# Local-window attention with a gated MLP on one core: the scores of two head pairs made by four 64x64 products a block

## The chip, the cores and the metric

The kernel runs on one core of one Trainium2 chip. The metric is the device time of one execution in microseconds (us). TensorE (PE) does the matrix products, VectorE (DVE) and ScalarE (ACT) the elementwise work, GpSimd (POOL) a little of it, and SyncE (SP) issues the loads and stores.

## The reference

Everything is fp32 in HBM. B = 4 batches, H = 8 heads, S = 768 positions, D = 64, DM = 512, DF = 512.

```python
# attention: a band of +-15 positions, and 24 block summaries (block = 32)
k_sum = k.reshape(B, H, 24, 32, D).max(axis=3)
v_sum = v.reshape(B, H, 24, 32, D).mean(axis=3)
scores_l = scale * q @ k.T                   # masked to |i - j| < 16
scores_s = scale * q @ k_sum.T + log(32)     # all 24 summaries
a = softmax(concat[scores_l, scores_s])
x = a @ concat[v, v_sum]                     # heads side by side: (B, S, 512)
# MLP with a spatial gate
h = relu(x @ w_in); u, v = h[..., :512], h[..., 512:]
v_n = (v - mean(v)) / sqrt(var(v) + 1e-6)    # over the 512 features
v_s = w_spatial @ v_n + b_spatial            # over the 768 positions
out = (u * v_s) @ w_out
```

## The kernel before

**Attention.** A query block is 64 positions (QB), and it sees KW = 120 columns: 64 + 32 keys around it and the 24 summaries, which lie in the key tile beside each segment. A unit of work is one batch, one chunk of 256 positions (four blocks, BPU) and one pair of heads; two units make a group, so that there are 4 x 3 x 2 = 24 groups. A pair's queries and keys lie one head in partitions 0 to 63 and the other in 64 to 127. Each unit goes through these steps:

- `scores` (product at L410): for each of four blocks and each head `a`, a product of 64 query rows (the stationary operand) with 120 key columns. Head `a` uses rows 64a to 64a+63 of TensorE's array and, since its output goes to PSUM partitions 64a to 64a+63, the same columns. So a unit has eight products, on two of the array's four 64x64 quarters, and fills one PSUM bank (tile `s`, 480 of 512 columns). Two such tiles exist (`s=2` in `SLOTS`).
- softmax: per block a DVE operation (L419: mask, scale, row minimum; it is listed with the read of its accumulator) and an ACT exponential (L423); then the sums' inverse (L428, L429) and a scaling of the whole tile (L431, on DVE or POOL).
- `trans` (L442): four transposes into tile `t`, copied to `pt` (L229, on ACT or DVE).
- `mix` (L458): for a whole group, 16 products of the values `ve` with the transposed weights, 64x64 each, in tile `x`. ACT makes the rounded high part `xh` (L471), DVE the remainder `xl` (L472).

**The MLP.** Each fp32 operand is a sum of two parts that TensorE takes at full rate, high and low, and each product is three (`mm3`, L491). In the order of a batch: `pv` (the half of `w_in` that is normalised) for six row tiles, `pu` (the other half) for four column tiles and two position ranges, `sp` (the spatial product) for four column tiles and two position ranges, and `po` (output) for six row tiles. DVE, ACT and POOL split the weights `win` (L262 to L284), `wsp` (L242, L243) and `wo` during batch 0, normalise `pv` (L518 to L530, result `vnh`, `vnl`) and gate `sp` (L553, L554, L562, L563; results `gt`, `gu`), which `po` reads.

**What sets the order.** Nothing is scheduled by hand on the engines. Each step is given to a planner (`Plan.add`) with its engines, an estimated duration, a priority and what it reads and writes. `Plan.order` picks, again and again, the operation that can start first (ties by priority) and so writes one order for each engine, which the engines keep. Tiles with few buffers (`SLOTS`) are handed out in turn (`TURNS`). Attention groups have priorities a `PACE` apart, the MLP's pieces follow each other from `DENSE_0` on, and the weights' priorities are `WIN_V`, `WIN_U`, `WSP_AT` and `WO_AT`. `FAVOUR` and `BUSY` say how long and how strongly POOL is preferred to DVE. While TensorE waits by the plan, before a marked point in group 1, the kernel fills in small `warm` products (L662).

Of the kernel before, what the change touches and what calls it, by code (L numbers as in the profile page):

```python
# [9 lines left out]
F32 = mybir.dt.float32  # L10
# [10 lines left out]
P = 128  # L21
# [4 lines left out]
QB = 64  # L26
# [37 lines left out]
class Plan:  # L64


    SLOTS = dict(s=2, t=1, x=1, m=4, k=4, vt=1, p=4, pt=3, x01h=2, x01l=2, x2h=2, x2l=2, g=NG, e=3, u=1, vnh=1, vnl=1,
                 gm=2, st=8, bs=4, mv=4)
    TURNS = ("s", "t", "x", "k", "vt", "p", "pt", "gm", "e")
    LAG = dict(PE=250, ACT=150, DVE=150, POOL=150, SP=0)  # L70

    def __init__(self):
# [106 lines left out]
def tile_local_summary_attention_gmlp(ctx: ExitStack, tc: tile.TileContext, qT, kext, vpad, vnat, vT, w_in, w_sp, b_rep, w_out, maskc, out):  # L179
# [39 lines left out]
    def early(name):  # L219
        return EARLY.get(name, 0.0)  # L220
# [176 lines left out]

    p_sb, pt_sb = {}, {}

    def scores(u, pri):  # L400
        b, c, pr = u
        ps = Buf(ps_s, [P, 512], F32, "s", f"s{b}_{c}_{pr}")
        kt, (qt, buf) = k_sb[b, pr], q_sb.pop(u)

        def mm(e):
            for i in range(BPU):
                g = c * BPU + i
                for a in range(2):
                    hs = slice(a * D, (a + 1) * D)
                    nc.tensor.matmul(  # L410
                        out=ps.t[hs, i * KW:(i + 1) * KW], lhsT=qt[hs, i], rhs=kt.t[hs, g * SEG:g * SEG + KW],
                        start=True, stop=True)
        add(("PE", 930), mm, pri, w=[ps], r=[kt, f"q{buf}"])
        pt = p_sb[u] = Buf(att, [P, BPU, KW], F32, "p", f"p{b}_{c}_{pr}")
        st = Buf(sums, None, None, "st", f"st{b}_{c}_{pr}")
        for i in range(BPU):
            g = c * BPU + i
            mi = 0 if g == 0 else (2 if g == NSEG - 1 else 1)
            add(("DVE", 205), lambda e, i=i, mi=mi: nc.vector.tensor_tensor_reduce(  # L419
                out=pt.t[:, i, :], in0=ps.t[:, i * KW:(i + 1) * KW], in1=mask[:, mi, :],  # L420
                scale=-1.0 / D ** 0.5, scalar=3e38, op0=ALU.add, op1=ALU.min,
                accum_out=st.t[:, 0, i:i + 1]), pri, w=[(pt, i)], r=[ps, "mask", pt, st])
# [8 lines left out]
        add(dict(DVE=590, POOL=1080), lambda e: eng(e).tensor_tensor(  # L431
            out=pt.t, in0=pt.t, in1=st.t[:, 0, :BPU].unsqueeze(2).broadcast_to([P, BPU, KW]), op=ALU.mult), pri,
            w=[(pt, "n")], r=[(pt, "i"), st, pt], port=True)

    def trans(u, pri):
        b, c, pr = u
        ps = Buf(ps_t, [P, 512], F32, "t", f"t{b}_{c}_{pr}")
        pt = p_sb.pop(u)

        def mm(e):  # L440
            for i in range(BPU):
                nc.tensor.transpose(out=ps.t[:KW, i * P:(i + 1) * P], in_=pt.t[:, i, :], identity=ident)  # L442
        add(("PE", 450), mm, pri, w=[ps], r=[(pt, "n"), pt])
        tt = pt_sb[u] = Buf(att, [KW, BPU * P], F32, "pt", f"pt{b}_{c}_{pr}")
        add(dict(ACT=510, DVE=600), lambda e: copy(e, tt.t, ps.t[:KW]), pri, w=[tt], r=[ps])

    xt, xh, xl, x2 = {}, {}, {}, {}

    def mix(b, c, g, buf, pri):
        ps = Buf(ps_x, [P, 2, CH], F32, "x", f"x{b}_{c}_{g}")  # L450
        tts = [pt_sb.pop((b, c, 2 * g + r)) for r in range(2)]

        def mm(e):
            for r in range(2):
                for n in range(BPU):
                    for a in range(2):
                        o = r * P + a * D
                        nc.tensor.matmul(  # L458
                            out=ps.t[a * D:(a + 1) * D, r, n * QB:(n + 1) * QB],
                            lhsT=ve[buf][:, n, o:o + D],  # L460
                            rhs=tts[r].t[:, n * P + a * QB:n * P + (a + 1) * QB],
                            start=True, stop=True)
        add(("PE", 1300), mm, pri, w=[ps], r=[*tts, f"vea{buf}", f"veb{buf}", f"ves{buf}_0", f"ves{buf}_1"])
        if c == 0:
# [78 lines left out]
    def spatial(b, th, d, pri):  # L543
        s = batch_state(b)
        ps = Buf(ps_m, [P, 512], F32, "m", f"sp{b}_{th}_{d}")
        ts = slice(0, 2 * TH) if th == 0 else slice(2 * TH, S)
        n = ts.stop - ts.start
        ds = slice(d * P, (d + 1) * P)
        vh, vl, u = s["vh"], s["vl"], s["u"]
        mm3(ps, n, [((lambda k=k: vh.t[:, k, ds], lambda k=k: vl.t[:, k, ds], lambda k=k: wsp_h[:, k, ts], lambda k=k: wsp_l[:, k, ts]),  # L550
                     [vh, vl, (vh, k), (vl, k), f"ws{k}_{ts.start}h", f"ws{k}_{ts.start}l"]) for k in range(NT)], pri)
# [3 lines left out]
        gt = Buf(moe, [P, 2 * TH], F32R, "g", f"gt{b}_{th}_{d}")  # L555
# [7 lines left out]
        add(two_ns(n), lambda e: eng(e).tensor_sub(out=gl[1](), in0=g.t[:, :n], in1=gh[1]()), pri, w=[kl], r=[g, kh, gt, gl[0]], port=True)  # L563
        s["gh"][th, d], s["gl"][th, d] = (*gh, kh), (*gl, kl)
# [40 lines left out]
    def attention(i):  # L605
# [68 lines left out]
VT_OFF, VM_OFF, KP_OFF = 7.67, 6.61, -9.44
# [74 lines left out]
```

## Time and profile before

| | |
|---|---|
| median of 3 runs | 435.26 us (435.07 to 436.68) |
| profiled execution, its own time | 436.41 us |
| its span, first to last instruction | 434.6 us |
| TensorE busy | 425.7 us, 98% of the span |
| VectorE busy | 265.6 us, 61% |
| ScalarE busy | 221.7 us, 51% |
| GpSimd busy | 45.6 us, 10% |
| granted TensorE clock, mean | 0.995 |

The busy time of TensorE is that of pipelined products whose ends are modelled, so the distance from one start to the next tells more than a duration. The span lies inside the profiled execution's time; the 1.8 us around it belong to no instruction. Each fp32 product of the code (L410, L458, L363, L662) is two MATMUL instructions in the trace; a transpose (L442) and a product of split operands (L491) is one.

### The profile page before, as it was taken

To read this page: it belongs to the slowest core of one execution; us is meant where nothing else is said; L and a number is where in the kernel's file an instruction comes from. 1 tells how busy PE (TensorE), PEld (TensorE's weight loads), DVE (VectorE), ACT (ScalarE), POOL (GpSimd) and SP (SyncE) were. 2 spreads that over 40 slices of the span, in tenths; PEclk is the share of its full clock that TensorE was granted. 3 is DMA by queue.
4 is the path that set the end of the run, shared out by engine and by line. 5 is a ranking of instruction groups with operands and counts; after the bars stand their busy time and mean duration, and the time that the engine had idled before them with its cause. 6 is when DMAs were issued, how large, how long until landed. Compare 5 with 4: busy or idle time off the path is not lost.

```text
span 434.6 us, 8979 instructions
## 1 busy us (share of the span) xinstructions
PE 425.7 (98%) x3374; PEld 353.7 (81%) x3374; DVE 265.6 (61%) x921; ACT 221.7 (51%) x668; POOL 45.6 (10%) x65
## 2 busy tenths in 40 slices
PE   8979999999999999999999999999999999999996
PEld 7637787788898888888888988789788988898885
DVE  4858999989993948455581657365482437143322
ACT  5658985874574546554273346375263254231121
POOL 1033611210001013010000002100000002010000
PEclk9989999999999999999999999999999999999999
DMA  8998967242155832320143251102103000000021
GB/s 288 362 271 289 296 205 247 76 133 60 26 165 161 250 118 60 106 67 26 38 144 118 87 186 27 38 24 62 38 26 109 26 36 15 0 2 0 2 97 48
DMA packets 25867, 47.03 MB, mean 108 GB/s; under 512 B 2528, under 2 KB 12896, under 8 KB 25696
## 3 DMA queue, kind: packets, MB, share of 16 engines
q1 hardware_dynamic: 25680, 46.33, 33.7%
q8 instruction: 26, 0.43, 0.4%
q14 instruction: 17, 0.14, 0.1%
q10 hardware_dynamic: 144, 0.13, 0.1%
HBM read 40.16 MB, written 6.29 MB: 107 GB/s over the span
## 4 chain that ended last, share of the span: by engine, by line
PE 82%; DMA 8%; DVE 8%; SPq 1%; issue 0%; ACT 0%; ACTq 0%
PE sp L491 24%; PE po L491 15%; PE pu L491 13%; PE pv L491 12%; PE s L410 8%; PE x L458 4%; PE t L442 4%; DMA vn<-in_vnat_dram 3%; DMA k<-in_kext_dram 2%; PE vsum L363 2%; DMA qd<-in_qT_dram 1%; DMA vt<-in_vT_dram 1%; DMA ws<-in_w_sp_dram 1%; DVE gm L342 1%; DVE p L419 1%; DVE p L431 1%
## 5 line engine op out<-in xcount | busy, mean ns | idle before, releaser
L423 ACT ACTIVATE p<-p,sums 128x120 f32<-128x120 f32 x192 | 73.6, 386 | 8.0 <-DVE sums L419 7.8
L491 PE MATMUL sp<-wsp_h,vnh 128*128 128x512 f32 (+1 forms) x192 | 66.7, 348 | 0.0
L491 PE MATMUL sp<-wsp_l,vnh 128*128 128x512 f32 (+1 forms) x192 | 64.7, 337 | 0.0
L491 PE MATMUL sp<-wsp_h,vnl 128*128 128x512 f32 (+1 forms) x192 | 64.6, 336 | 0.0
L419 DVE CUSTOM_DVE_ANT_0 p<-s,mask 128x120 f32<-128x120 f32 x192 | 42.8, 276 | 12.4 <-PE s L410 12.2
L491 PE MATMUL po<-wo_h,gt 128*128 128x512 f32 x128 | 47.7, 402 | 0.0
L410 PE MATMUL s<-k,qd 64*64 64x120 f32 x768 | 45.9, 267 | 0.5 <-DMA qd<-in_qT_dram 0.5
L410 PEld LDWEIGHTS s<-k,qd 64*64 64x64 f32 x768 | 39.1, 133 | 7.7 <-issue 4.4
L491 PE MATMUL pu<-xh,win_h 128*128 128x512 f32 (+1 forms) x128 | 44.7, 349 | 0.0
L491 PE MATMUL pu<-xh,win_l 128*128 128x512 f32 (+1 forms) x128 | 43.1, 337 | 0.0
L491 PE MATMUL pu<-xl,win_h 128*128 128x512 f32 (+1 forms) x128 | 43.1, 336 | 0.0
L562 ACT CAST gt<-g 128x512 fp32r<-128x512 f32 (+1 forms) x32 | 16.3, 513 | 50.2 <-DVE g L554 50.1
L491 PEld LDWEIGHTS sp<-wsp_h,vnh 128*128 128x128 f32 x192 | 36.4, 189 | 5.1 <-issue 1.3
L491 PE MATMUL pv<-win_h,xh 128*128 128x512 f32 x96 | 39.8, 414 | 0.0
L491 PEld LDWEIGHTS sp<-wsp_h,vnl 128*128 128x128 f32 x192 | 36.4, 189 | 3.9
L472 DVE TENSOR_TENSOR xl<-x,xh 128x512 fp32r<-128x512 f32 x24 | 16.4, 685 | 37.7 <-ACT xh L471 37.7
L491 PEld LDWEIGHTS sp<-wsp_l,vnh 128*128 128x128 f32 x192 | 36.4, 190 | 3.5
L491 PE MATMUL pv<-win_l,xh 128*128 128x512 f32 x96 | 37.6, 391 | 0.0
L491 PE MATMUL pv<-win_h,xl 128*128 128x512 f32 x96 | 37.5, 391 | 0.0
L491 PE MATMUL po<-wo_l,gt 128*128 128x512 f32 x96 | 37.5, 391 | 0.0
L553 DVE TENSOR_TENSOR g<-sp,brep 128x512 f32<-128x512 f32 (+1 forms) x32 | 17.7, 554 | 31.5 <-PE sp L491 22.1
L229 ACT COPY pt<-t 120x512 f32<-120x512 f32 x40 | 23.4, 584 | 26.1 <-PE t L442 25.9
(103 smaller groups left out, 784.7 us busy)
## 6 DMA issues: line engine op xcount, KB each, us to landing
k<-in_kext_dram SPq DMA_DIRECT2D x16, 544.0 KB, 5.8
qd<-in_qT_dram SPq DMA_DIRECT2D x24, 256.0 KB, 4.2
ve<-in_vpad_dram SPq DMA_DIRECT2D x24, 256.0 KB, 3.7
out_dram<-ob SPq DMA_DIRECT2D x23, 256.0 KB, 2.0
vt<-in_vT_dram SPq DMA_DIRECT2D x12, 384.0 KB, 4.0
wi<-in_w_in_dram SPq DMA_DIRECT2D x6, 512.0 KB, 5.1
ve<-in_vpad_dram SPq DMA_DIRECT2D x24, 128.0 KB, 3.4
wo<-in_w_out_dram SPq DMA_DIRECT2D x8, 256.0 KB, 5.4
```

The costliest lines, as they stand in the source:

```text
L229: (nc.scalar.copy if e == "ACT" else nc.vector.tensor_copy)(out=out_, in_=in_)
L342: nc.vector.tensor_reduce(out=g[:, :48].rearrange("p (s g) -> p s g", g=4), in_=kv[:, :, :QB].rearrange("p s (g e) -> p s g e", e=16), axi ...
L363: add(("PE", 860), lambda e, t=t, o=o: nc.tensor.matmul(out=ps.t[:SEG], lhsT=vs_in[:, o:o + SEG], rhs=vn.t[:, t, :], start=t == 0, stop=t ...
L410: nc.tensor.matmul(out=ps.t[hs, i * KW:(i + 1) * KW], lhsT=qt[hs, i], rhs=kt.t[hs, g * SEG:g * SEG + KW], start=True, stop=True)
L419: add(("DVE", 205), lambda e, i=i, mi=mi: nc.vector.tensor_tensor_reduce(out=pt.t[:, i, :], in0=ps.t[:, i * KW:(i + 1) * KW], in1=mask[:, ...
L423: add(("ACT", 380), lambda e, i=i: nc.scalar.activation(out=pt.t[:, i, :], in_=pt.t[:, i, :], func=AF.Exp, scale=-1.0, bias=st.t[:, 0, i:i ...
L442: nc.tensor.transpose(out=ps.t[:KW, i * P:(i + 1) * P], in_=pt.t[:, i, :], identity=ident)
L458: nc.tensor.matmul(out=ps.t[a * D:(a + 1) * D, r, n * QB:(n + 1) * QB], lhsT=ve[buf][:, n, o:o + D], rhs=tts[r].t[:, n * P + a * QB:n * P ...
L472: add(("DVE", 610), lambda e: nc.vector.tensor_sub(out=l.t[:, :, fs], in0=ps.t, in1=h.t[:, :, fs]), pri, w=[kl], r=[ps, kh, h, l])
L491: nc.tensor.matmul(out=ps.t[:, :n], lhsT=x, rhs=y, start=(j == i == 0), stop=(j == last and i == 2))
L553: add(("DVE", dve_ns(n)), lambda e: nc.vector.tensor_add(out=g.t[:, :n], in0=ps.t[:, :n], in1=brep[:, ts]), pri, w=[g], r=[ps, "brep"])
L562: add(("ACT", act_ns(n)), lambda e: nc.scalar.copy(out=gh[1](), in_=g.t[:, :n]), pri, w=[kh], r=[g, gt])
```

## The change

`scores` now makes a whole group at once. For each block it issues four products in the order (head 0, pair 0), (head 1, pair 1), (head 0, pair 1), (head 1, pair 0): the head `a` picks the 64 rows of the array and the PSUM bank, the pair `r` the 64 columns, that is the PSUM partitions. The tile `s` is two banks wide and there is one of it (`s=1`) in place of two of one bank, so PSUM use stays. Softmax and transpose work on one bank, that is on one head of both pairs, and `mix` picks its columns the other way round; their number and shapes stay.

Beside that, the planner's numbers are new: ten staging buffers in place of eight (`NG`), the priorities and the two numbers for POOL, and staging buffers of weights and outputs that are handed out without turn. A second-half `sp` now takes its result's buffer before its products, and those of `d >= 2` follow the first half's gated tiles.

```diff
-NG = 8
+NG = 10
...
-    SLOTS = dict(s=2, t=1, x=1, m=4, k=4, vt=1, p=4, pt=3, ...
+    SLOTS = dict(s=1, t=1, x=1, m=4, k=4, vt=1, p=4, pt=3, ...
...
-    def scores(u, pri):
-        b, c, pr = u
-        ps = Buf(ps_s, [P, 512], F32, "s", f"s{b}_{c}_{pr}")
-        kt, (qt, buf) = k_sb[b, pr], q_sb.pop(u)
+    def scores(b, c, pg, buf, pri):
+        ps = Buf(ps_s, [P, 2, 512], F32, "s", f"s{b}_{c}_{pg}")
+        kts = [k_sb[b, 2 * pg + r] for r in range(2)]
+        qt = qd[buf]
 
         def mm(e):
             for i in range(BPU):
                 g = c * BPU + i
-                for a in range(2):
+                for a, r in ((0, 0), (1, 1), (0, 1), (1, 0)):
                     hs = slice(a * D, (a + 1) * D)
                     nc.tensor.matmul(
-                        out=ps.t[hs, i * KW:(i + 1) * KW], lhsT=qt[hs, i], rhs=kt.t[hs, g * SEG:g * SEG + KW],
-                        start=True, stop=True)
-        add(("PE", 930), mm, pri, w=[ps], r=[kt, f"q{buf}"])
+                        out=ps.t[r * QB:(r + 1) * QB, a, i * KW:(i + 1) * KW], lhsT=qt[hs, r, i],
+                        rhs=kts[r].t[hs, g * SEG:g * SEG + KW], start=True, stop=True)
+        add(("PE", 1000), mm, pri, w=[ps], r=[*kts, f"q{buf}"])
+        for a in range(2):
+            softmax((b, c, pg, a), ps, pri)
...
-                out=pt.t[:, i, :], in0=ps.t[:, i * KW:(i + 1) * KW], in1=mask[:, mi, :],
+                out=pt.t[:, i, :], in0=ps.t[:, a, i * KW:(i + 1) * KW], in1=mask[:, mi, :],
...
-                            rhs=tts[r].t[:, n * P + a * QB:n * P + (a + 1) * QB],
+                            rhs=tts[a].t[:, n * P + r * QB:n * P + (r + 1) * QB],
...
-WIN_V, WIN_U, WSP_AT, WO_AT = -7.07, 47.63, 54.52, 99.2
+WIN_V, WIN_U, WSP_AT, WO_AT = -6.93, 37.2, 100.98, 115.53
...
-FAVOUR, BUSY = 1380.0, 44480.0
+FAVOUR, BUSY = 570.0, 43570.0
```

TensorE's order at the first scores of batch 2, which stand before and after in much the same place of the program. Names are tile, batch, chunk and pair (after: pair group); `k2_0` and `k2_1` are the keys of two pairs, `qd0` the queries of both. Before:

```order
L491 MATMUL pv1_2_2076<-win_h_99,xl1_01_1_1343 128x512
L410 MATMUL s2_0_0_2098<-k2_0_1633,qd0_105 64x120 x8
L410 MATMUL s2_0_1_2115<-k2_1_1640,qd0_105 64x120 x8
L380 MATMUL vmp2_0_2125<-ident_82,vs_in_93 88x128
L380 MATMUL vmp2_1_2127<-ident_82,vs_in_93 88x128
L491 MATMUL pv1_3_2129<-win_h_99,xh1_01_0_1193 128x512
```

After:

```order
L497 MATMUL sp0_1_3_1918<-wsp_h_101,vnl0_941 128x256
L411 MATMUL s2_0_0_1954<-k2_0_1629,qd0_105 64x120
L411 MATMUL s2_0_0_1954<-k2_1_1635,qd0_105 64x120 x2
L411 MATMUL s2_0_0_1954<-k2_0_1629,qd0_105 64x120 x2
L411 MATMUL s2_0_0_1954<-k2_1_1635,qd0_105 64x120 x2
L411 MATMUL s2_0_0_1954<-k2_0_1629,qd0_105 64x120 x2
```

Sixteen products stand there in both; the two keys now alternate, and one tile takes the place of two. The group also stands further forward: ahead of batch 1's first `pv`, where it stood behind the third.

DVE's order just before the first output product of batch 0 (`po0_0`), which reads the gated tiles `gu0_0_0` to `gu0_0_3`. `p1_2_0` is a softmax step of the group whose scores were made last. Before:

```order
L553 TENSOR_TENSOR g0_0_3_1618<-sp0_0_3_1465,brep_88 128x512
L431 TENSOR_TENSOR p1_1_2_1556<-p1_1_2_1556,sums_91 128x480
L472 TENSOR_TENSOR xl1_01_0_1208<-x1_1_0_1577,xh1_01_0_1193 128x2x256
L554 TENSOR_TENSOR g0_0_3_1618<-g0_0_3_1618,u0_928 128x512
L428 TENSOR_SCALAR sums_91<-sums_91 128x5
L429 RECIPROCAL sums_91<-sums_91 128x4
L229 COPY pt1_1_2_1663<-t1_1_2_1648 120x512
L431 TENSOR_TENSOR p1_1_3_1598<-p1_1_3_1598,sums_91 128x480
L563 TENSOR_TENSOR gu0_0_3_1675<-g0_0_3_1618,gt0_0_3_1658 128x512
L419 ISA p1_2_0_1684,sums_91<-s1_2_0_1603,mask_87 128x120
```

After:

```order
L437 TENSOR_TENSOR p1_1_1_1_1566<-p1_1_1_1_1566,sums_91 128x480
L562 TENSOR_TENSOR g0_0_2_1622<-g0_0_2_1622,u0_918 128x512
L561 TENSOR_TENSOR g0_0_3_1644<-sp0_0_3_1554,brep_88 128x512
L425 ISA p1_2_0_0_1653,sums_91<-s1_2_0_1603,mask_87 128x120
L425 ISA sums_91 128x1
L562 TENSOR_TENSOR g0_0_3_1644<-g0_0_3_1644,u0_918 128x512
L570 TENSOR_TENSOR gu0_0_2_1668<-g0_0_2_1622,gt0_0_2_1646 128x512
```

After, four softmax steps of the group `s1_2_0` stand ahead of `gu0_0_3`, of which this shows the first; before, that group's steps all stand behind it. Counted from the start of the program to `gu0_0_3`, DVE's order has 398 operations before and 397 after: four more softmax steps (each with the read of its accumulator), one more sum over `vt`, and one more `win` piece of each of two steps; and, since POOL takes them, two fewer scalings of `p`, two fewer `vnl`, three fewer `wf`, one fewer `wo` and four fewer `wsp` remainders.

More of the change, by code (lines that the diff above doesn't have):

```diff
@@ L64 @@
 class Plan:
-    SLOTS = dict(s=2, t=1, x=1, m=4, k=4, vt=1, p=4, pt=3, x01h=2, x01l=2, x2h=2, x2l=2, g=NG, e=3, u=1, vnh=1, vnl=1,
+    SLOTS = dict(s=1, t=1, x=1, m=4, k=4, vt=1, p=4, pt=3, x01h=2, x01l=2, x2h=2, x2l=2, g=NG, e=3, u=1, vnh=1, vnl=1,
                  gm=2, st=8, bs=4, mv=4)
     TURNS = ("s", "t", "x", "k", "vt", "p", "pt", "gm", "e")
+    OUT_OF_TURN = ("wi", "wf", "wo", "ws", "ob")
     LAG = dict(PE=250, ACT=150, DVE=150, POOL=150, SP=0)
@@ L95, in add @@
         for x in (*w, *r):
-            if isinstance(x, Buf) and not x.ops and x.tag in self.TURNS and x.args[4][0] != "w" and x.args[4][:3] != "vmp":
+            if isinstance(x, Buf) and not x.ops and x.tag in self.TURNS and x.args[4][:2] not in self.OUT_OF_TURN :
                 self.turn.setdefault(x.tag, []).append(x)
@@ L326, in wo_load @@
             split64(st, 0, f, 0, wo_v[c][:, fs], wo_h[:, c, fs], wo_l[:, c, fs], pri, f"wo{c}_{o}")
-    k_sb, q_sb = {}, {}
+    k_sb = {}
     def key_load(b, pr, pri):
@@ L387, in q_load @@
         dma(qd[buf], qT[b, c, g], 256, pri, w=[f"q{buf}"])
-        for r in range(2):
-            q_sb[b, c, 2 * g + r] = (qd[buf][:, r], buf)
     def v_load(b, c, g, buf, pri):
@@ L407, in mm, with softmax @@
                 g = c * BPU + i
-                for a in range(2):
+                for a, r in ((0, 0), (1, 1), (0, 1), (1, 0)):
                     hs = slice(a * D, (a + 1) * D)
                     nc.tensor.matmul(
-                        out=ps.t[hs, i * KW:(i + 1) * KW], lhsT=qt[hs, i], rhs=kt.t[hs, g * SEG:g * SEG + KW],
-                        start=True, stop=True)
-        add(("PE", 930), mm, pri, w=[ps], r=[kt, f"q{buf}"])
-        pt = p_sb[u] = Buf(att, [P, BPU, KW], F32, "p", f"p{b}_{c}_{pr}")
-        st = Buf(sums, None, None, "st", f"st{b}_{c}_{pr}")
+                        out=ps.t[r * QB:(r + 1) * QB, a, i * KW:(i + 1) * KW], lhsT=qt[hs, r, i],
[3 more added lines that the diff above has]
+            softmax((b, c, pg, a), ps, pri)
+    def softmax(u, ps, pri):
+        b, c, pg, a = u
+        pt = p_sb[u] = Buf(att, [P, BPU, KW], F32, "p", f"p{b}_{c}_{pg}_{a}")
+        st = Buf(sums, None, None, "st", f"st{b}_{c}_{pg}_{a}")
         for i in range(BPU):
@@ L435, in trans @@
     def trans(u, pri):
-        b, c, pr = u
-        ps = Buf(ps_t, [P, 512], F32, "t", f"t{b}_{c}_{pr}")
+        b, c, pg, a = u
+        ps = Buf(ps_t, [P, 512], F32, "t", f"t{b}_{c}_{pg}_{a}")
         pt = p_sb.pop(u)
@@ L450, in mix @@
         ps = Buf(ps_x, [P, 2, CH], F32, "x", f"x{b}_{c}_{g}")
-        tts = [pt_sb.pop((b, c, 2 * g + r)) for r in range(2)]
+        tts = [pt_sb.pop((b, c, g, a)) for a in range(2)]
         def mm(e):
@@ L549, in spatial @@
         vh, vl, u = s["vh"], s["vl"], s["u"]
+        gt = Buf(moe, [P, 2 * TH], F32R, "g", f"gt{b}_{th}_{d}")
         mm3(ps, n, [((lambda k=k: vh.t[:, k, ds], lambda k=k: vl.t[:, k, ds], lambda k=k: wsp_h[:, k, ts], lambda k=k: wsp_l[:, k, ts]),
-                     [vh, vl, (vh, k), (vl, k), f"ws{k}_{ts.start}h", f"ws{k}_{ts.start}l"]) for k in range(NT)], pri)
+                     [vh, vl, (vh, k), (vl, k), f"ws{k}_{ts.start}h", f"ws{k}_{ts.start}l"]) for k in range(NT)], pri, *([gt] if th else []),
+            *([s["gl"][0, j][2] for j in range(NC)] if th and d >= NG - 8 else []))
         g = Buf(moe, [P, DF], F32, "e", f"g{b}_{th}_{d}")
@@ L617, in attention @@
                 key_prep(b, 2 * g + r, pri + KP_OFF + early(f"p{b}{g}{r}"))
-        for r in range(2):
-            scores((b, c, 2 * g + r), pri + early(f"s{i}{r}"))
+        scores(b, c, g, buf, pri)
         if b == c == g == 0:
@@ L625, in attention @@
         for r in range(2):
-            trans((b, c, 2 * g + r), pri + early(f"t{i}{r}"))
+            trans((b, c, g, r), pri)
         mix(b, c, g, buf, pri + early(f"x{i}"))
@@ L670, in tile_local_summary_attention_gmlp @@
         seen = len(traced)
[L674 to L676 removed]
+PACE_0, PACE, DENSE_0, STRETCH = 11.97, 16.23, 67.63, 1.35
+WIN_V, WIN_U, WSP_AT, WO_AT = -6.93, 37.2, 100.98, 115.53
+VT_OFF, VM_OFF, KP_OFF = 6.65, 8.21, 2.58
 WARM, WARM_TO = 1 / 330, 1
```

3 lines of the change are left out of this document (1 added, 2 removed).

## The prediction

> **What bounds the kernel now.** I read the busy time first, then the waits of TensorE, then the busy time by stretches, and last the time line of single products. The page's first part and the waits of TensorE (engine, line, waited for: us in total, times, longest):
>
> ```profile
> PE 425.7 (98%) x3374; PEld 353.7 (81%) x3374; DVE 265.6 (61%) x921; ACT 221.7 (51%) x668; POOL 45.6 (10%) x65
> ```
>
> ```profile
> PE vsum L363 <- DMA vn<-in_vnat_dram: 2.4, 1, 2.4
> PE warm L596 <- POOL ident masks.py:199: 1.8, 1, 1.8
> PE s L410 <- DMA qd<-in_qT_dram: 0.5, 1, 0.5
> PE vmp L380 <- DVE vs_in L376: 0.2, 1, 0.2
> PE t L442 <- POOL p L431: 0.2, 1, 0.2
> ```
>
> TensorE waits 5 us in all, so its work sets the time, except at the start. The stretches, for all engines and then for the instructions of L410 alone:
>
> ```profile
> core 0: us, PE busy (x) PEld busy (x) DVE busy (x) ACT busy (x) POOL busy (x), PEclk, DMA share, GB/s
> 0.00:45.00 45.00, 40.24 (x347) 29.19 (x348) 30.25 (x132) 30.37 (x96) 11.24 (x23) 0.96 0.93 302
> 45.00:130.00 85.00, 84.51 (x769) 70.12 (x769) 81.32 (x287) 60.53 (x193) 13.31 (x15) 1.00 0.48 149
> 130.00:400.00 270.00, 270.00 (x2092) 227.61 (x2093) 143.90 (x484) 124.72 (x370) 21.01 (x27) 1.00 0.23 71
> ```
>
> ```profile
> 0.00:45.00 45.00, 9.72 (x160) 8.15 (x160) 0.96 0.93 302
> 45.00:130.00 85.00, 11.36 (x192) 9.77 (x192) 1.00 0.48 149
> 130.00:434.60 304.60, 24.80 (x416) 21.14 (x416) 1.00 0.22 68
> ```
>
> There are three stages. Up to 45 us the DMA engines are busy 93% of the time and TensorE is fed by what lands; part of its busy time is warm-up filling. From 45 to 130 us TensorE is full, and DVE is too: 81.3 of 85 us. After 130 us TensorE alone is full, DVE at 53%. A group's scores are 32 MATMULs (16 products of two), so 160, 192 and 416 of them are 5, 6 and 13 groups.
>
> **The price of a group's scores.** The time line (start us, duration us, engine, line) of two units in a row, of one unit alone, of a group's `x`, of warm-up products on the whole array, and of the first 20 ns of the two units:
>
> ```profile
> 143.69 1.04 PE L410 MATMUL s<-k,qd 64*64 64x120 f32 x16
> 144.66 0.39 PE L491 MATMUL sp<-wsp_h,vnh 128*128 128x256 f32 x1
> ```
>
> ```profile
> 164.12 1.86 PE L410 MATMUL s<-k,qd 64*64 64x120 f32 x32
> 165.91 0.42 PE L380 MATMUL vmp<-ident,vs_in 128*88 128x128 f32 x2
> ```
>
> ```profile
> 256.36 1.15 PE L458 MATMUL x<-pt,ve 120*64 120x64 f32 x32
> 257.44 0.50 PE L491 MATMUL pv<-win_h,xh 128*128 128x512 f32 x1
> ```
>
> ```profile
> 11.43 0.60 PE L662 MATMUL warm<-ident 128*128 128x120 f32 x4
> 11.87 0.60 PE L277 MATMUL wwi<-wi,ident 128*128 128x512 f32 x1
> ```
>
> ```profile
> 164.12 0.32 PE L410 MATMUL s<-k,qd 64*64 64x120 f32 x2
> ```
>
> From start to start, 16 instructions take 0.97 us and 32 take 1.79: so 0.82 us for 16 more, 0.1025 for two, and a fixed 0.15 for the change of form at both ends. On the whole array one instruction of 120 columns takes 0.44/4 = 0.11. So two quarters of the array work at the same time, each at full rate, and both start within the first 20 ns. The `x` products do it too: by the same 0.15, 0.058 us for two of 64 columns, where one on the whole array would take 0.11 x 64/120 = 0.059. There both halves of the columns share their rows, each with its own moving data.
>
> The change lets four quarters work: 32 instructions in 8 steps of 0.1025 plus 0.15 = 0.97 us. The bounds are 0.97 and 1.79 (no more than two at once; no row shows four, and none shows two quarters that share columns and differ in rows). I take 0.97: two at once cost nothing in either direction, and weight loads are no limit that I can see, since `x` issues 32 loads and 32 products in 1.08 us, which would make it 1.08 at most. The Trainium skill's page "TensorEngine Tiling (Array Packing)", section "Tiling Modes", says that the four 64x64 tiles load and multiply independently; by that the price is 0.97 as well, and the trace bears it out for two of them.
>
> A group saves 1.79 - 0.97 = 0.82 us. Where the two units stood apart before (five groups by the order, among them the one at 143.69) it saves 0.15 more. The scores of 24 groups fall by 24 x 0.82 + 5 x 0.15 = 20.4 us. What of this reaches the end is worked out by stage.
>
> **Up to 45 us.** Five groups, of which two stood apart: 5 x 0.82 + 2 x 0.15 = 4.4 us. Here loads are late:
>
> ```profile
> 3.12 9.08 DMA k<-in_kext_dram
> 12.21 14.01 DMA vn<-in_vnat_dram
> ```
>
> These two pieces of the chain that ended last take 23 us, and `vsum`, for which TensorE stands still 2.4 us (above), is the next piece. The queue of loads is the same in the new order up to and beyond `vn`. The first scores come later (both wait for the fourth `wwi`, and DVE prepares the keys behind more of the weights' split), the planner fills 84 warm-up instructions instead of 62, and `pv0_0` is reached behind the same steps. I count 0; the bounds are 4.4 us gained and 22 x 0.11 = 2.4 lost.
>
> **From 45 to 130 us.** Six groups and one that stood apart: TensorE sheds 6 x 0.82 + 0.15 = 5.1 us. But DVE has little slack, so what DVE sheds decides. Its rows, of the step before `po0_0` and of two forms by group:
>
> ```profile
> 125.61 0.65 DVE L431 TENSOR_TENSOR p<-p,sums 128x480 f32<-128x480 f32 x1
> 126.18 0.68 DVE L563 TENSOR_TENSOR gu<-g,gt 128x512 fp32r<-128x512 f32 x1
> 126.78 0.27 DVE L419 CUSTOM_DVE_ANT_0 p<-s,mask 128x120 f32<-128x120 f32 x1
> 126.98 0.08 DVE L419 DVE_READ_ACCUMULATOR2_ANT sums<- 128x1 f32 x1
> 126.98 0.28 DVE L419 CUSTOM_DVE_ANT_0 p<-s,mask 128x120 f32<-128x120 f32 x1
> ```
>
> ```profile
> L376 DVE TENSOR_REDUCE vs_in<-vt 128x24 f32<-128x768 f32 x12 | 11.4, 948 | 8.5 <-DMA vt<-in_vT_dram 8.3
> L243 DVE TENSOR_TENSOR wsp_l<-ws,wsp_h 128x256 fp32r<-128x256 f32 x6 | 2.5, 418 | 0.3 <-ACT wsp_h L242 0.3
> ```
>
> From start to start a scaling of `p` costs 0.57 us, a 512-wide operation 0.60, a softmax step 0.20; a sum over `vt` 0.95; a 256-wide operation, 0.418 from start to end, 0.37 by the share that 0.60 has of 0.68 (an estimate). Up to `gu0_0_3` the new order has on DVE 4 x 0.20 + 0.95 + 2 x 0.60 = 2.95 us more and 2 x 0.57 + 2 x 0.60 + 8 x 0.37 = 5.3 less: 2.4 us less. Its 3.7 us of idle time here may shrink by some. So this stage gains between 2.4 and 5.1 us; with DVE nearly full I take 2.7, closer to its own end. What then stands late on TensorE are transposes and scores of batch 1, which wait for DVE.
>
> **After 130 us.** Thirteen groups, of which two stood apart: 13 x 0.82 + 2 x 0.15 = 11.0 us, and TensorE has no second bound here: DVE's 53% and ACT's 46% leave room for work to come 4% faster. The single two-bank tile costs nothing as long as a group's eight softmax steps, 1.6 us by the 0.20 above, end before the next group's scores. The closest two here, `s1_2_1` and `s2_0_0`, have 36 half-width `sp` products between them, 0.12 us each from start to start, 4.3 in all:
>
> ```profile
> 125.04 0.28 PE L491 MATMUL sp<-wsp_h,vnl 128*128 128x256 f32 x1
> 125.16 0.28 PE L491 MATMUL sp<-wsp_h,vnh 128*128 128x256 f32 x1
> ```
>
> The new `sp` holds and the ten staging buffers are covered by the same room.
>
> Sum: 0 + 2.7 + 11.0 = 13.7 us off the profiled execution's 436.41 (span 434.6 and 1.8 around it) gives 422.7; the median of the runs lies 1.15 under that execution, so 421.6 us.
>
> **The rivals.** (A) DVE gives way entirely: POOL and ACT take enough, or its idle time closes. For it speaks that TensorE waited for DVE hardly at all (0.2 us), against it that 3.7 us of slack are all there is. Then 5.1 + 11.0 = 16.1 us: 419.2. With 2.7 of the start's 4.4 as well, 416.5.
>
> (B) One score tile makes DVE's lateness a stall. Before `po0_0` DVE is late: it starts on a group's first softmax step at 126.78, whose scores started at:
>
> ```profile
> 121.76 1.86 PE L410 MATMUL s<-k,qd 64*64 64x120 f32 x32
> 123.54 0.38 PE L491 MATMUL sp<-wsp_h,vnh 128*128 128x256 f32 x1
> ```
>
> The unit was done near 122.6, so DVE lags 4.2 us. In the new order 27 half-width `pu` products stand between the scores of `s1_0_1` and `s1_1_0`, and no more to `s1_1_1`. At 0.12 that is 3.2 us. With a lag of 4.2 and 1.6 for eight steps TensorE waits 2.6 us, twice, with everything queued behind: 5 us, so 426.6. DVE's lag there, in the new order, is not shown.
>
> (C) No more than two at once. Each product is two MATMULs on the same quarter, one behind the other in the built program. If TensorE starts strictly in that order, the second waits 0.1025 us for the first, the next quarter's first starts beside it, and two are at work however many quarters there are: 16 or 17 steps, 1.79 to 1.89 us. Past 45 us only the 3 x 0.15 of separate units remain: 435.26 - 0.45 = 434.8, no change. Against it: in a strict order the first MATMUL of a unit would run alone for one step, and the row of the first 20 ns has two. For it: nothing here shows three. The Trainium skill's "TensorE: Matmul & The Clock Gate", sections "Step-by-step: what each phase is for" and "The mechanism", states this strict order for products, with only weight loads pulled ahead; if it holds across quarters, this rival's time comes out and not mine.
>
> (D) Slower: changing from one diagonal pair of quarters to the other drains the array like a change of form. A group changes seven times within itself; at up to 0.15 us each its scores cost 16 x 0.1025 + 8 x 0.15 = 2.84, 1.05 more than now, on 19 groups past 45 us 20 us: 455. It decides as soon as a change costs more than some 0.02 us (19 x 7 x 0.02 = 2.7). Against it, all four are of one form, and a drain shows in the trace only where the form changes.
>
> **How the numbers follow.** The forecast has 0.49, (A) 0.19, (B) 0.13, (C) 0.14, (D) 0.05. About 0.5%, 2.2 us, is what a measurement of this kernel can tell from no change. Forecast, (A) and (B) are faster by more: 0.81. (C) is mostly no change, 0.10, with 0.04 slower, since the order was laid out for short scores; with (D), slower is 0.09. The range leaves out (C) and (D), 0.19 in all: from 416.5, (A) with part of the start, to 430.0, (B) with scores at `x`'s 1.08 us (19 x 0.11 = 2.1) and a little of the start's 2.4 lost.
>
> **What would show it.** Right: from the start of a group's scores to the next line's start 0.97 us, with 8 starts of four; the first `pv` near 45 us; DVE still near full up to 130 us with small waits of TensorE for it, and none later. Wrong: 1.8 us a group (C), over 2 (D), or long waits of `s` or `t` for DVE between 80 and 130 us (B).

## The result, and the profile after

The changed kernel takes 417.37 us (median of 4 runs, 417.02 to 418.28), the kernel before 435.16 beside it (433.29 to 436.68): a ratio of 0.9596 with a 95% interval of 0.9555 to 0.9637, or 17.8 us less. The profiled execution took 417.61 us, its span is 415.8. Ratios here and below leave out single executions that took over 1.5% longer than the fastest of the same kernel, which is one of `e3`; medians and ranges hold them.

Busy time and the waits of TensorE, in the same views as before:

```profile
PE 406.2 (98%) x3396; PEld 336.7 (81%) x3396; DVE 261.7 (63%) x914; ACT 219.2 (53%) x667; POOL 51.9 (12%) x73
```

```profile
PE warm L603 <- POOL ident masks.py:199: 1.8, 1, 1.8
PE t L448 <- ACT pt L230: 1.3, 2, 1.0
PE t L448 <- DVE p L437: 1.2, 2, 0.9
PE s L411 <- DVE sums L425: 0.9, 2, 0.6
PE s L411 <- ACT p L429: 0.6, 1, 0.6
PE s L411 <- issue: 0.2, 1, 0.2
```

TensorE has 19.5 us less work and is as full as it was. No wait for a load is left; in their place stand small waits of transposes and scores for VectorE and ScalarE. The stretches, for all engines and then for the scores alone (the line is now L411):

```profile
0.00:45.00 45.00, 41.70 (x445) 31.05 (x445) 34.60 (x149) 32.89 (x109) 15.65 (x28) 1.00 0.99 339
45.00:130.00 85.00, 82.32 (x778) 67.97 (x775) 80.83 (x276) 61.47 (x192) 19.20 (x22) 1.00 0.49 150
130.00:400.00 270.00, 270.00 (x2110) 227.21 (x2109) 143.32 (x486) 122.23 (x362) 17.03 (x24) 1.00 0.21 67
```

```profile
0.00:45.00 45.00, 6.36 (x192) 5.16 (x192) 1.00 0.99 339
45.00:130.00 85.00, 5.33 (x164) 4.11 (x160) 1.00 0.49 150
130.00:415.80 285.80, 13.67 (x416) 10.69 (x416) 1.00 0.21 67
```

Past 130 us TensorE does not stop (270 of 270 us), as before; between 45 and 130 us it stands still for 2.7 us where it was 0.5. One group in the time line, its first 30 ns, and the products that had begun in each of the first three steps:

```profile
164.95 1.05 PE L411 MATMUL s<-k,qd 64*64 64x120 f32 x32
165.93 0.42 PE L381 MATMUL vmp<-ident,vs_in 128*88 128x128 f32 x2
```

```profile
164.95 0.33 PE L411 MATMUL s<-k,qd 64*64 64x120 f32 x4
```

```profile
164.94:165.06 0.12, 0.11 (x4) 0.11 (x8) 1.00 0.00 0
165.06:165.17 0.11, 0.11 (x8) 0.11 (x12) 1.00 0.00 0
165.17:165.27 0.10, 0.10 (x12) 0.10 (x8) 1.00 0.00 0
```

Thirty-two instructions take 0.98 us from start to start, against 1.79 for the same thirty-two before. Four begin together, 7 ns apart, and each step adds four; from the second step on, the steps in the trace lie 0.1025 us apart. So four quarters of the array work at once. Of the 24 groups 21 take 0.98 us; the other three, all before 45 us, take 1.04 to 1.29.

Where the 17.8 us come from is read from two points that both kernels pass with the same 160 and 352 score instructions behind them: the first `pv` and the first `po`. Here are the first `pv` of the kernel before, of the changed one, and of two more profiled executions of the kernel before (spans 435.7 and 431.7 us, times 437.44 and 433.52), then the first `po` in the same order:

```profile
44.67 0.50 PE L491 MATMUL pv<-win_h,xh 128*128 128x512 f32 x1
```

```profile
40.12 0.48 PE L497 MATMUL pv<-win_h,xh 128*128 128x512 f32 x1
```

```profile
43.70 0.80 PE L491 MATMUL pv<-win_h,xh 128*128 128x512 f32 x1
```

```profile
41.91 0.50 PE L491 MATMUL pv<-win_h,xh 128*128 128x512 f32 x1
```

```profile
127.67 0.48 PE L491 MATMUL po<-wo_h,gt 128*128 128x512 f32 x1
```

```profile
120.38 0.40 PE L497 MATMUL po<-wo_h,gt 128*128 128x512 f32 x1
```

```profile
128.73 0.48 PE L491 MATMUL po<-wo_h,gt 128*128 128x512 f32 x1
```

```profile
124.53 0.48 PE L491 MATMUL po<-wo_h,gt 128*128 128x512 f32 x1
```

From the first `po` to the end of the span the kernel before needs 306.9, 307.0 and 307.2 us, the changed one 295.4: 11.5 us less, or up to 11.8. Between the two points it needs 83.0, 85.0 and 82.6, the changed one 80.3: 2.7 us less than the profiled execution of the prediction, and 4.8 and 2.4 less than the other two. Up to the first `pv` it is 1.8 to 4.6 us less. So executions of the kernel before agree behind the first `po` and differ by some us ahead of it.

### The profile page after: what moved, and what is told of

It reads as the page before. It is cut to its first block, busy times and chain, and to the rows that moved or that the text cites. A ratio compares the mean times of both kernels' runs of the same rounds, so it can differ in the third digit from the quotient of the medians.

```text
span 415.8 us, 9020 instructions
## 1 busy us (share of the span) xinstructions
PE 406.2 (98%) x3396; PEld 336.7 (81%) x3396; DVE 261.7 (63%) x914; ACT 219.2 (53%) x667; POOL 51.9 (12%) x73
## 4 chain that ended last, share of the span: by engine, by line
PE 82%; DVE 8%; ACT 6%; DMA 2%; issue 1%; POOL 0%; SPq 0%; DVEq 0%; ACTq 0%; POOLq 0%
PE sp L497 25%; PE po L497 16%; PE pv L497 12%; PE pu L497 12%; PE x L464 4%; PE s L411 4%; PE t L448 4%; ACT p L429 4%; PE warm L668 2%; DMA wo<-in_w_out_dram 1%; DMA ws<-in_w_sp_dram 1%; PE wwi L280 1%; PE wwi L278 1%; DVE gm L343 1%; DVE p L425 1%
## 5 line engine op out<-in xcount | busy, mean ns | idle before, releaser
L497 PE MATMUL po<-wo_h,gt 128*128 128x512 f32 x128 | 46.7, 399 | 0.0
L531 POOL TENSOR_TENSOR mv<-mv,mhalf 128x1 f32<-128x1 f32 x24 | 16.3, 679 | 175.2 <-DVE mv L529 160.3
L429 ACT ACTIVATION_READ_ACCUMULATOR p<-p,sums 128x1 f32 x192 | 36.6, 191 | 0.0
L527 DVE BATCH_NORM_STATS2 mv<-vf 128x6 f32<-128x512 f32 x24 | 16.6, 690 | 29.1 <-ACT vf L524 29.0
```

Of the source, the lines that this page charges most:

```text
L429: add(("ACT", 380), lambda e, i=i: nc.scalar.activation(out=pt.t[:, i, :], in_=pt.t[:, i, :], func=AF.Exp, scale=-1.0, bias=st.t[:, 0, i:i ...
L497: nc.tensor.matmul(out=ps.t[:, :n], lhsT=x, rhs=y, start=(j == i == 0), stop=(j == last and i == 2))
L527: nc.vector.bn_stats(out=mv.t[:, 2:], in_=vf.t)
L531: add(("POOL", 500), lambda e: nc.gpsimd.tensor_tensor(out=mv.t[:, 1:2], in0=mv.t[:, 1:2], in1=mhalf, op=ALU.pow), pri, w=[mv])
```

## The experiments

### The four quarters: the order of a group's products

`e1_pair_by_pair`: the same sixteen products, but one diagonal pair of quarters for all four blocks, and then the other.

```diff
-            for i in range(BPU):
-                g = c * BPU + i
-                for a, r in ((0, 0), (1, 1), (0, 1), (1, 0)):
+            for two in (((0, 0), (1, 1)), ((0, 1), (1, 0))):
+                for i in range(BPU):
+                    g = c * BPU + i
+                    for a, r in two:
...
```

> The changed kernel with the sixteen products of a group in another sequence: first the pair of quarters (head 0, pair 0) and (head 1, pair 1) for all four blocks, then the other pair of quarters for all four blocks. Everything else, the order on all engines too, stays. Theory (four quarters at work at once make the gain): only two are within reach, a group's scores take 16 steps of 0.1025 and 0.15, 1.79 us in place of 0.98, and 19 groups past the start add 15.4 us, of which up to 2.7 fills waits for VectorE: 430 to 433 us. Rival (the new order and the earlier start make the gain, not the four quarters): within 2 us of 417.4. Rival (TensorE looks far ahead past a product whose quarter is busy): the group stays near 0.98 us and the time near 417.4.

`e2_quarter_by_quarter`: the loop over the quarters outside, that over the blocks inside.

```diff
-            for i in range(BPU):
-                g = c * BPU + i
-                for a, r in ((0, 0), (1, 1), (0, 1), (1, 0)):
-                    hs = slice(a * D, (a + 1) * D)
+            for a, r in ((0, 0), (1, 1), (0, 1), (1, 0)):
+                hs = slice(a * D, (a + 1) * D)
+                for i in range(BPU):
+                    g = c * BPU + i
```

> The changed kernel with the four products of one quarter (eight MATMULs) side by side before the next quarter's. Everything else stays. Theory, with a look-ahead of about one product per quarter: nearly one at a time, some 29 steps of 0.1025 and 0.15, 3.1 us a group, and 19 groups past the start add 40 us: 450 to 460 us. Rival (each quarter has its own queue, deep enough for eight): 0.98 us a group and 417.4. Rival (strict order of starts, the two MATMULs of a product included): 29 steps or more as well, but then the changed kernel itself could not have reached 0.98, which its time line shows; this rival has fallen already.

Measured: 426.07 us for `e1` (425.43 to 426.67; ratio to the kernel before 0.9781, 0.9742 to 0.982) and 447.61 for `e2` (446.9 to 448.0; 1.0274, 1.0233 to 1.0315). One group of `e1`, and one of `e2` with the first 0.46 us of another:

```profile
200.22 1.51 PE L412 MATMUL s<-k,qd 64*64 64x120 f32 x32
201.66 0.50 PE L498 MATMUL sp<-wsp_h,vnh 128*128 128x512 f32 x1
```

```profile
198.70 2.43 PE L411 MATMUL s<-k,qd 64*64 64x120 f32 x32
201.06 0.39 PE L497 MATMUL pu<-xh,win_h 128*128 128x256 f32 x1
```

```profile
213.15:213.61 0.46, 0.46 (x4) 0.46 (x5) 1.00 0.00 0
```

A group takes 0.98, 1.44 and 2.36 us by nothing but the order of its products. Behind the first `po`, where 13 groups stand and TensorE is full, `e1` needs 6.0 us more than the changed kernel and `e2` 17.9: 13 x 0.46 and 13 x 1.38. Between the first `pv` and the first `po`, with six groups, it is 1.9 and 6.6 us more, less than 6 x 0.46 = 2.8 and 6 x 1.38 = 8.3; the rest, 1.2 and 5.7 us, lies up to the first `pv`. Both expectations missed in size: for `e1` I had 1.79 us a group and 430 to 433 us, for `e2` 3.1 us and 450 to 460.

The starts tell how TensorE takes them. No record of the trace names the quarter; which start belongs to which is read from the program's order and from the distance of 0.1025 us between starts on the same quarter. In `e2` a quarter gets eight instructions in a row. The first quarter's start at 213.152, 213.305, 213.407, 213.510 and 213.612 us, the second quarter's first at 213.618, and the first quarter's other three after that, at 213.715, 213.817 and 213.920. So an instruction for a free quarter does pass earlier ones that wait for a busy quarter, in both runs only once no more than three wait there: with a fourth, all that was behind it was held up. In `e1` the next pair of quarters begins 13 ns after the fifth start of the first quarter (200.678 and 200.691), again with three left. My numbers held the reach to be shorter than it is. Whether the limit lies with the products or with their weight loads, these runs do not tell.

The strict order of rival (C) falls with this. The Trainium skill, "TensorE: Matmul & The Clock Gate", "Step-by-step: what each phase is for", says that products stay in program order and only weight loads are pulled ahead; the starts above do not agree with it across quarters of the array. Within one quarter the records look alike and do not tell.

### The parts apart: the new scores, the new numbers

`e3_new_scores_old_numbers`: the changed kernel with the planner's numbers of before.

```diff
-NG = 10
+NG = 8
...
-PACE_0, PACE, DENSE_0, STRETCH = 11.97, 16.23, 67.63, 1.35
-WIN_V, WIN_U, WSP_AT, WO_AT = -6.93, 37.2, 100.98, 115.53
-VT_OFF, VM_OFF, KP_OFF = 6.65, 8.21, 2.58
+PACE_0, PACE, DENSE_0, STRETCH = 12.13, 15.91, 66.3, 1.27
+WIN_V, WIN_U, WSP_AT, WO_AT = -7.07, 47.63, 54.52, 99.2
+VT_OFF, VM_OFF, KP_OFF = 7.67, 6.61, -9.44
...
-FAVOUR, BUSY = 570.0, 43570.0
+FAVOUR, BUSY = 1380.0, 44480.0
```

> The changed kernel with the planner's numbers of before (priorities, eight staging buffers, preference for GpSimd); the scores by four quarters stay. Theory (the scores carry the gain past the start): group scores at 0.98 us and 418 to 424 us, the rest of the difference being waits for VectorE between 45 and 130 us. Rival (the new numbers carry it): 430 us or more.

One thing more changes with `NG`: the condition of the hold is `d >= NG - 8`, so that with eight buffers all four second-half `sp` follow the first half's gated tiles, and not only those of `d >= 2`. This holds for `e7` and `e10` below, too.

`e4_old_scores_new_numbers`: the kernel before with all of the change but the scores: the numbers, the rules for turns and `sp`'s holds.

```diff
-NG = 8
+NG = 10
...
+    OUT_OF_TURN = ("wi", "wf", "wo", "ws", "ob")
...
-                     [vh, vl, (vh, k), (vl, k), f"ws{k}_{ts.start}h", f"ws{k}_{ts.start}l"]) for k in range(NT)], pri)
+                     [vh, vl, (vh, k), (vl, k), f"ws{k}_{ts.start}h", f"ws{k}_{ts.start}l"]) for k in range(NT)], pri, *([gt] if th else []),
+            *([s["gl"][0, j][2] for j in range(NC)] if th and d >= NG - 8 else []))
...
-WIN_V, WIN_U, WSP_AT, WO_AT = -7.07, 47.63, 54.52, 99.2
+WIN_V, WIN_U, WSP_AT, WO_AT = -6.93, 37.2, 100.98, 115.53
...
-FAVOUR, BUSY = 1380.0, 44480.0
+FAVOUR, BUSY = 570.0, 43570.0
```

> The kernel before with the planner's numbers, the ten staging buffers and the rules for turns of the changed kernel; its scores stay two quarters at a time, with two one-bank tiles. Theory: TensorE has its old work, so 432 to 437 us; what it gains against 435.2 is what the order alone is worth at the start. Rival (the new numbers carry the gain): 420 to 425 us.

Measured: 431.79 us for `e3` (429.42 to 437.7; ratio 0.9884, 0.9818 to 0.9949) and 434.91 for `e4` (434.04 to 436.37; 1.0005, 0.9977 to 1.0032), the kernel before 434.9 beside them. The short scores with the old numbers bring some 3 us by the medians (5 by the ratio), where I had expected 11 to 17; the new numbers alone bring nothing, both together 17.8. Waits of TensorE between 45 and 130 us in `e3`, and that stretch (`vmp` is the transpose of the values' block sums `vs_in`):

```profile
PE vmp L381 <- DVE vs_in L377: 2.6, 1, 2.6
PE t L448 <- DVE p L437: 2.3, 2, 1.8
PE t L448 <- ACT p L429: 1.6, 1, 1.6
PE s L411 <- issue: 1.1, 1, 1.1
```

```profile
45.00:130.00 85.00, 75.38 (x680) 60.39 (x679) 79.44 (x282) 58.53 (x184) 10.85 (x13) 0.96 0.45 136
```

With short scores in the order that the planner makes of the old numbers, TensorE comes too early for what VectorE and ScalarE hand it, and stands still 9.6 of 85 us. Besides, its clock is granted at 0.96 here: it falls to half twice, at 97.98 and 125.29 us, each time shortly after such waits. In `e4` TensorE is full (84.0 of 85 us here), and an order cannot shorten what is full.

### The kernel before twice more, and a lighter VectorE

`e5_before_again` and `e5_before_third` are the kernel before, unchanged (437.44 and 433.52 us). They stand for the scatter of its start.

> The kernel before, unchanged, for a second profile of its first 45 us. If the late landing of vn (14.0 us after its issue) and the half clock after it belong to this kernel's order, vsum starts again near 26 us and pv near 44.7. Rival (the landing scatters from run to run): vn lands near 23.6 us, as in the other kernels, vsum starts near 24 and pv near 41 to 42.

> The kernel before, unchanged, for a third profile, with the same expectations as for the second.

Their rows are among those of the result. What TensorE waits for up to 45 us differs each time, in the kernel before always a load: in the profiled execution of the prediction 2.4 us for `vn` and 0.5 for `qd`; in the second 2.3 for `qd`; in the third 1.8 for `qd` and 0.6 for `vn`. In the first two 3.41 us at half clock follow. The late landing of `vn` thus scatters, but waits of this kind go with the order: in all seven traces that have both the short scores and the new pace of the attention (the changed kernel, `e1`, `e2`, `e6`, `e8`, `e9` and `e10`) TensorE waits neither for `vn` nor for `qd`, in each of the seven others (the kernel before three times, `e3`, `e4`, `e7` and `e11`) for one or both, 1.3 us or more in all.

`e6_lighter_vector` is the changed kernel, and `e7_lighter_vector_old_numbers` is `e3`, each with shorter reads in two of VectorE's reductions: the block maxima leave out 12 of each 16 keys and the block sums 24 of each 32 values, so that the output is not that of the reference.

```diff
-                in_=kv[:, :, :QB].rearrange("p s (g e) -> p s g e", e=16),
+                in_=kv[:, :, :QB].rearrange("p s (g e) -> p s g e", e=16)[:, :, :, :4],
...
-            out=vs[:, QB:], in_=vt.t.rearrange("p (n e) -> p n e", e=SBLK),
+            out=vs[:, QB:], in_=vt.t.rearrange("p (n e) -> p n e", e=SBLK)[:, :, :8],
```

> The changed kernel with less work on VectorE and the same order everywhere: the block maxima read 4 of each 16 keys and the block sums 8 of each 32 values, so that each of these reductions takes about 0.25 us in place of 0.95; eight or nine of them lie between 45 and 130 us, 6 us in all. Theory (VectorE paces TensorE there): TensorE's 2.7 us of idle time in that stage go, and with them 1.5 to 3 us of the time: 414.5 to 416. Rival (TensorE waits there for chains of single steps, not for a full VectorE): under 1 us.

> The new scores with the planner's numbers of before, and the same relief of VectorE as in the run before this one. Theory (the new scores alone gain little because VectorE is full between 45 and 130 us): 5 to 8 us less than the 431.8 us without the relief. Rival (the old numbers put the steps in an order in which TensorE waits for them whatever VectorE's load): under 2 us less.

Measured: 417.76 us for `e6` (416.67 to 422.23; ratio 0.9635, 0.9572 to 0.9699) and 429.38 for `e7` (427.75 to 432.28; 0.9871, 0.9821 to 0.9921). The middle of `e6`:

```profile
45.00:130.00 85.00, 83.05 (x794) 68.43 (x787) 75.89 (x275) 61.04 (x192) 18.69 (x22) 1.00 0.52 157
```

VectorE has 4.9 us less to do than in the changed kernel here, and the end does not move. `e7` lies 2.4 us under `e3` by the medians, where `e3` loses 14.4; the two ratios, 0.9871 and 0.9884, do not tell even that from nothing, and I had expected 5 to 8 us if VectorE's load counted. So how much VectorE has to do is not what holds TensorE up in these two orders; where a step stands in VectorE's order may be, and the next runs ask that.

### Which of the numbers

Four runs put back one kind of number each in the changed kernel, `e8`, `e9`, `e10` and `e11` in this order:

```diff
-FAVOUR, BUSY = 570.0, 43570.0
+FAVOUR, BUSY = 1380.0, 44480.0
```

```diff
-WIN_V, WIN_U, WSP_AT, WO_AT = -6.93, 37.2, 100.98, 115.53
+WIN_V, WIN_U, WSP_AT, WO_AT = -7.07, 47.63, 54.52, 99.2
```

```diff
-NG = 10
+NG = 8
```

```diff
-PACE_0, PACE, DENSE_0, STRETCH = 11.97, 16.23, 67.63, 1.35
+PACE_0, PACE, DENSE_0, STRETCH = 12.13, 15.91, 66.3, 1.27
...
-VT_OFF, VM_OFF, KP_OFF = 6.65, 8.21, 2.58
+VT_OFF, VM_OFF, KP_OFF = 7.67, 6.61, -9.44
```

> The changed kernel with only the two numbers for GpSimd (FAVOUR, BUSY) as they were before. Theory of the prediction, that the new numbers help in the middle because VectorE gives work to GpSimd: GpSimd busy near 46 instead of 52 us, VectorE 2 to 3 us more before the first output product, and 2 to 3 us lost: 419.5 to 420.5. Rival, that the numbers only fit together as one order for TensorE, and any of them put back makes new waits of it: 3 to 10 us lost, 420 to 428, with waits of TensorE for transposes and scores as in the kernel with all old numbers. Third, that these two numbers are of no account: 417 to 418.5.

> The changed kernel with only the priorities of the weights (WIN_V, WIN_U, WSP_AT, WO_AT) as they were before: the split of the spatial and output weights is asked for earlier, that of the second half of the input weight later. Theory that these carry what the new numbers bring, since the split is VectorE's and ScalarE's other work between 45 and 130 us and stands in the way of the softmax: 8 to 14 us lost, 425 to 431, with TensorE idle for 8 us or more between 45 and 130 us. Rival, that the numbers only fit together and each put back costs some: 420 to 428. Rival, that VectorE's share given to GpSimd carries it: 417 to 418.5 here.

> The changed kernel with eight staging buffers instead of ten (NG), all other numbers new. If the number of buffers carries the gain (loads and gated tiles wait for a free buffer with eight): 3 us or more lost, 420 and above, with loads issued later and waits of TensorE for DMA. If it is of no account for itself: 417 to 419. If any change of order costs: 420 to 428 with waits for VectorE and ScalarE and not for DMA.

> The changed kernel with only the pace of the attention groups and the offsets of the values and keys (PACE_0, PACE, DENSE_0, STRETCH, VT_OFF, VM_OFF, KP_OFF) as they were before. They say when the sums of the values are asked for, for which TensorE waited longest with all old numbers (2.6 us in one wait). If they carry it: 425 to 431 with that wait back. If the numbers only fit together: 420 to 428. If they are of no account: 417 to 419.

Measured, with the profiled span, what of it TensorE is not busy (span less busy time), and for how long its clock was granted at half before the last 4 us:

| | median us (runs) | span | TensorE not busy | half clock |
|---|---|---|---|---|
| changed kernel | 417.37 (417.02 to 418.28) | 415.8 | 9.6 | 0 |
| `e8`, GpSimd's numbers | 417.88 (417.3 to 419.54) | 415.7 | 9.6 | 0 |
| `e11`, the attention's pace | 424.51 (422.71 to 425.08) | 423.2 | 14.4 | 6.83 |
| `e10`, eight buffers | 429.55 (428.96 to 432.54) | 427.9 | 17.2 | 6.83 |
| `e3`, all | 431.79 (429.42 to 437.7) | 430.2 | 19.2 | 6.83 |
| `e9`, the weights' priorities | 437.16 (433.3 to 439.84) | 435.7 | 24.3 | 20.48 |
| kernel before | 435.16 (433.29 to 436.68) | 434.6 | 8.9 | 3.41 |

Each span follows within 1.4 us from that of the changed kernel, 415.8, the added idle time, and half of the time at half clock: for `e11` 415.8 + 4.8 + 3.4 = 424.0, for `e10` 426.8, for `e3` 428.8. For `e9`, where 9.6 of the 20.5 us fall into the waits themselves, 415.8 + 14.7 + 5.4 = 435.9. So all of them have the short scores and lose them again as idle time and half clock of TensorE. The losses do not add up: `e9` alone loses more than `e3`, which has all of the old numbers. The rules for turns and for `sp`'s holds were not put back alone in any run.

In `e9` one wait is most of it. It stands among the first `sp` of batch 0, at a transpose of attention weights that VectorE has still to scale; more `sp` are queued behind it. Here are the time line of TensorE, and VectorE's work in these 13.8 us by line (busy us in all and mean ns of one, then idle time ahead of it):

```profile
98.30 0.40 PE L497 MATMUL sp<-wsp_h,vnl 128*128 128x512 f32 x1
112.49 1.08 PE L448 MATMUL t<-ident,p 128*120 128x128 f32 x4 [13.80 <-DVE p L437]
```

```profile
L284 DVE TENSOR_TENSOR wf<-wf,wo_h 128x256 f32<-128x256 f32 x6 | 2.5, 420 | 0.0
L270 DVE SCALAR_TENSOR_TENSOR wo<-wo 128x256 f32<-128x256 uint32 x5 | 2.1, 421 | 0.0
L285 DVE TENSOR_TENSOR wo_l<-wf,wo 128x256 fp32r<-128x256 f32 x5 | 2.1, 419 | 0.0
L265 DVE SCALAR_TENSOR_TENSOR wf<-wo,wf 128x256 int32<-128x256 int32 x5 | 2.0, 420 | 0.0
...
L264 DVE TENSOR_SCALAR wf<-wf 128x256 int32<-128x256 int32 x5 | 1.4, 289 | 0.0
L268 DVE TENSOR_SCALAR wo<-wf 128x256 int32<-128x256 int32 x5 | 1.4, 289 | 0.0
...
L437 DVE TENSOR_TENSOR p<-p,sums 128x480 f32<-128x480 f32 x1 | 0.7, 652 | 0.0
```

Thirty-one steps of the split of `wo`, 11.5 us, stand in VectorE's order ahead of the one scaling, 0.65 us, for which TensorE waits; the output products that read `wo` begin only at 138.4. VectorE is busy for 13.7 of the 13.8 us, and does the wrong work first. `e8` says that GpSimd's two numbers are of no account, and against my expectation GpSimd has more to do with the old ones (55.2 us busy, not 46). `e9` missed my 425 to 431 us on the far side. `e11` lies in the 420 to 428 us of numbers that only fit together; `e10` lost more than that, but without the waits for loads that I had named for the buffers themselves. What in `e10` holds TensorE up is shown in part only: its waits are scattered over ScalarE (3.2 us for `p` in all) and "issue", which names nothing, and the longer hold of `sp` that comes with eight buffers is not told apart from the buffers.

## Why the prediction came out, point by point

**A group's scores.** Forecast 0.97 us in eight steps of four, measured 0.98 in eight steps of four. The step and the fixed part hold, and as far as these rows show quarters that share columns or rows do not slow each other. (C) and (D) fall by the same rows; a change between diagonal pairs costs nothing that shows.

**After 130 us.** Forecast 11.0 us, measured 11.5 behind the first `po`. The prediction counted two groups with separate units there; the trace of the kernel before has three (from 143.7, 220.9 and 321.2 us on), which makes it 11.1. The starts of the scores to the next instruction's start, added up behind the first `po`, are 23.7 us before and 12.8 after: 10.9 us less. The rest is other work: twelve half-width `sp` products more and one group's `x` less stand behind that point now (12 x 0.12 more, 1.08 less), and the transposes, in other surroundings, take 0.7 us less from start to start. TensorE waits nowhere in this stretch, as foreseen; one score tile of two banks and the new holds of `sp` cost nothing there.

**From 45 to 130 us.** Forecast 2.7 us, measured 2.7 against the profiled execution of the prediction (4.8 and 2.4 against the other two), but the step that gave the number is not borne out. I took VectorE's own relief, 2.4 us, for what decides. The balance of TensorE is the better account: it sheds about 5, and waits 2.7 instead of 0.5. The waits are those that I named, of transposes and scores, and VectorE stays near full (80.8 of 85 us). But `e6` takes twice that relief off VectorE and gains nothing, and `e8` moves work between VectorE and GpSimd without effect. That the number came so near was luck.

**Up to 45 us.** Here the forecast missed a term: 0 against 4.6 in the two profiled executions, or 1.8 and 3.6 by the other two profiles of before. The first `pv` came at 40.1 us and not near 45. "Here loads are late" was true of the kernel before, for which `vsum`'s wait of 2.43 us and the half clock behind it are one case of three. It does not follow that TensorE's shorter work is lost there. `vn`, which took 14.0 us then, landed after 10.3 in the changed kernel:

```profile
DMA to landing us min/median/max: 10.3/10.3/10.3
```

and `vsum` started at 23.89 us without a wait of TensorE; in the other two profiles of the kernel before it started at 24.0, once after a wait of 0.6 us. After that the loads were in time, so what TensorE shed did count. The two bounds that I gave, 4.4 us shed by five groups and 2.4 spent on 22 more warm-up instructions, were no alternatives: both came (66 warm-up instructions before, 88 after), 2.0 us net. The rest is waits for loads that the new order does not have (3.0 us less 1.6 of new small waits) and 1.7 for 3.41 us at half clock. Counted in this way, with the prices of the prediction and not measured share by share, it is 5.1 us against 4.6.

**The sum.** 4.6 + 2.7 + 11.5 = 18.8 us of span, against 0 + 2.7 + 11.0 forecast; the missing term is the start. Rival (A)'s 419.2 lies nearer, and its 416.5 with part of the start's gain nearest of all. The start did give that part and more, but the reason of (A) for the middle, that VectorE gives way, is not borne out: the middle gave 2.7 us and not 5.1. (B), one tile that makes VectorE's lateness a stall, did not come: the scores wait 0.4 us between 45 and 130 us.

**What the prediction did not ask** is what the change would be without its numbers. I counted their hold on TensorE's order as nothing to be gained or lost; `e3` shows that 14 of the 18 us are lost without them, though alone they bring nothing.

## What to carry to other kernels

Small products run side by side on TensorE when neighbours in its order go to different parts of the array; order them so that they alternate, since here four or more that waited for one part held up the rest. When TensorE is full and its work gets shorter, the saving may be there only once the other engines' orders are laid out anew for it, as it was here: look for a wait of TensorE behind which the engine it waits for is busy with something that is needed much later. An engine's total load does not tell that; the order of its work does.

## What the runs showed of the hardware beyond that

In the traces of this case TensorE's clock falls to half after waits of some 2 to 3 us, for 3.41 us or a multiple, and so charges a wait a second time. The three pieces around such a fall in `e3`, where TensorE had waited for 2.6 us until 95.33:

```profile
94.57:97.98 3.41, 1.92 (x35) 1.58 (x36) 3.41 (x10) 2.26 (x5) 0.00 (x0) 1.00 0.38 115
97.98:101.39 3.41, 3.41 (x10) 2.64 (x9) 3.41 (x13) 2.20 (x7) 1.09 (x1) 0.50 0.40 115
101.39:104.80 3.41, 3.41 (x17) 2.77 (x16) 3.41 (x13) 1.51 (x5) 0.00 (x0) 1.00 0.00 0
```

All stretches between two changes of the granted clock in the traces of this case are whole multiples of 3.413 us. The Trainium skill, "TensorE: Matmul & The Clock Gate", "What's actually happening", gives a free-running window of 3413 ns, which agrees, and at least one idle window as the condition for the fall, which does not if idle means that TensorE does nothing: here single waits of 2.2 to 2.8 us were followed by half clock within 3 us in five of six cases, and in `e10` waits of 1.5 and 1.0 us close together were enough, and in `e7` one of 1.9 us was, while others of up to 1.9 us had no such effect. In the 3.41 us ahead of the fall above TensorE was even busy for 1.92. Laid out on the grid of 3.413 us, the traces say more: each of the 13 windows at full clock with TensorE busy for less than 0.43 of it was followed by half clock, of 14 windows with 0.45 to 0.56 four were, and of the others, with more, none. What decides between 0.45 and 0.56, these runs do not settle.
